# Seven products for the third column group of a gated ffn's first layer, interleaved with the other two groups

## The chip, the cores and the metric

One NeuronCore of one Trainium2 chip runs the whole program. The metric is device time in microseconds (us). Three executions of the kernel before took 1438.28, 1441.61 and 1444.34 us; the median is 1441.61 us.

## The reference

Threshold attention over 8 batches x 8 heads, 576 positions, head width 64, and then a feed-forward block with a product of two linear branches over the 4608 resulting rows. All data is float32.

```python
scores = scale * np.matmul(q, k.transpose(0, 1, 3, 2))
thresh = np.max(scores, axis=-1, keepdims=True) - tau
scores = np.where(scores >= thresh, scores, -1000000000.0)
scores = scores - np.max(scores, axis=-1, keepdims=True)
attn = np.exp(scores)
attn = attn / (np.sum(attn, axis=-1, keepdims=True) + 1e-09)
attn_out = np.matmul(attn, v)
...
x = attn_out.transpose(0, 2, 1, 3).reshape(B * S, H * D)   # 4608 x 512
a = x @ w_a                                                # 512 -> 1536
b = x @ w_b
return a * b @ w_out                                       # 1536 -> 512
```

## The kernel before

**Units and blocks.** The attention is cut into 160 units. A unit `(i, u)` is a pair of heads of one batch and up to two tiles of 64 query rows for each head. `scores` (line 386) makes the score products of a unit in two PSUM tiles, VectorE takes the row maximum (L393), ScalarE makes bias and exponential (L413, L414), VectorE thresholds, multiplies and sums (L417); only then are the two PSUM tiles free. ScalarE normalises (L436), VectorE transposes 32x32 pieces (L480), and two DMAs by way of a DRAM scratch finish the transposition (`swap`, `wT`). Three units later `weighted` multiplies with v (L520), and ScalarE and VectorE copy the result into a tile of x (L527, L528). When 256 rows of x are complete they are a block; there are 18.

**The matmuls.** All are 64x64 tiles of the array, four at a time in its four quadrants. A float32 matmul shows as two records in the trace.

**ffn of a block.** The 1536 columns of the hidden layer are three groups of 512. The second and third group are tile `h1` of the hidden values, the first is tile `h0`. For 16 of the blocks (all but the first two, which are plain throughout) the two groups of `h1` are computed by `sevens_of` (matmuls at L680): x is split by rows and depth, the weights by depth and branch, and seven products of such quarters (128 rows, half the depth) stand in place of eight, with sums of the weights that were made once on GpSimd (`first_sums`, L641) and sums of x that are made for each block (`x_sums`, L550, four per tile of x, written into a tile `xU`). Products 1, 6, 7 and 4 accumulate one on the other in one PSUM pair `a`; between them the running value is copied out (L698, L705, L710) or used (L714). Products 5 and 3 do the same in a pair `b` (L719, L723), product 2 has a `b` of its own (L702). The columns of `h0` are computed plainly (L753): four steps of 256 rows x 128 columns x two branches, and each evicts with ScalarE (L759) or VectorE (L761). Three of the plain steps stand between products of the seven, so that 6 and 7, 7 and 4, 5 and 3 are never neighbours. The second layer (L810) also uses seven products; its sums of hidden values run on GpSimd (L779).

**Order.** Every engine's order is fixed when the program is written (`keep_order`). A loop over slots `g` emits a unit's steps and, between them, calls `advance`, which takes steps from the generator `ffn` as long as a budget of matmul columns lasts. So the matmuls of a block stand spread over about nine units, and evictions of the ffn stand in the queues of ScalarE and VectorE between the steps of the attention. After the last unit the remaining blocks run alone.

**Memory.** PSUM is one pool of four pairs of banks (`banks`); scores of a unit take two, every product, `pv` and `po` takes one. Tiles of x, their half-swapped copies `xS` and the sums `xU` come from one pool of `XT_BUFS` = 7; temporaries `osb` (the `u3` of product 7 and the outputs of the second layer) from `OSB_BUFS` = 4; v of a head pair from four buffers, loaded once per pair.

**DMA.** Nearly all DMAs are issued by SyncE in one queue. In the loop they are put in a list `bulk` by `post`, and `passed`/`pump` take them from it in proportion to the matmul columns issued (`PUMP`), each tied to a matmul already issued; `flush` issues whatever a consumer needs at once. Entries `tw` and `wT` overtake others.

Of the kernel before, what the change touches and what calls it, by code (L numbers as in the profile page):

```python
# [24 lines left out]
XT_BUFS = 7  # L25
Q_BUFS = 2
OSB_BUFS = 4
# [7 lines left out]
RAWS = 4  # L35
# [19 lines left out]
def kernel(  # L55
# [83 lines left out]
    def post(key, *moves):  # L139

        if not state["paced"]:
            for move in moves:
                nc.sync.dma_start(*move)  # L143
        else:
            at = len(bulk)
            if key[0] in ("tw", "wT"):
                while at and bulk[at - 1][0][0] not in ("tw", "wT") and bulk[at - 1][1] >= state["slot"] - 1:
                    at -= 1
            bulk.insert(at, (key, state["slot"], moves))
# [50 lines left out]
    def load_v(i, again=False):  # L200
        b, hp = pairs[i]
        if not again:
            loaded[i]["v"] = loads.tile([P, NSLOT, D], FP32, tag="vm", bufs=HP, name="vm")
        for j in range(2):
            rows, half = v[b, 2 * hp + j], loaded[i]["v"][j * D:(j + 1) * D]
            if i >= HP or again:
                if i < HP:
                    rows = rows.rearrange("(c s p) d -> p c s d", c=2, p=Q)
                else:
                    rows = rows.rearrange("(p c s) d -> p c s d", c=2, p=Q)  # L210
                post(("v", i), *((half[c * Q:(c + 1) * Q], rows[:, c]) for c in range(2)))
            else:
                nc.sync.dma_start(half, rows.rearrange("(s p) d -> p s d", p=D))
# [37 lines left out]
    more_sb = more_u32.bitcast(FP32)  # L251

# [17 lines left out]
    def convert_first(n):  # L270

        if n not in raws:
            return
        raw, top = raws[n], pieces[n][0]
        if n % (OSB_BUFS + 1) == OSB_BUFS:
            low = more_sb[:, 2 * QUARTER + P:2 * QUARTER + P + CW]
        else:
            low = work.tile([P, CW], FP32, tag="osb", bufs=OSB_BUFS, name="low")
        nc.scalar.activation(top, raw[:, :, 1].bitcast(FP32), AF.Abs)
        nc.scalar.activation(low, raw[:, :, 0], AF.Copy, bias=2.0, scale=2.0 ** -51)
        stages[n] = low  # L290
# [35 lines left out]
    rooms = [t.rearrange("p (n w) -> p n w", n=NR) for t in rooms]  # L326
    load_rows(0, "q", rooms[0])
# [217 lines left out]
    def x_sums(x):  # L545

        t = x_tile("xU").rearrange("p m (k n) -> p m k n", k=2)
        b11, b12, b21, b22 = (x[:, k * 2:k * 2 + 2, n * P:(n + 1) * P] for k in range(2) for n in range(2))
        for m, a, b in ((0, b12, b11), (1, b22, t[:, 0]), (2, b22, b12), (3, b21, t[:, 1])):
            nc.gpsimd.tensor_tensor(t[:, m], a, b, op=ALU.subtract)  # L550
        return t

    def exchange_blocks():
        while complete and not state["layer"] and not blocks:
            x, what = complete.pop(0)
            xs, done = ahead.pop(what[1:], (None, 0)) if what[0] == "half" else (None, 0)
            xs = xs or x_tile("xS")
            for hp in range(done, HP):
                exchange(x, xs, hp, 0, HALF, nc.gpsimd)
            blocks.append(((x, xs) + ((x_sums(x), x_sums(xs)) if state["first"] >= 3 * SEVENS else ()), what))  # L560
# [70 lines left out]

    def first_sums(n, group):

        quarter = [w[:, NG - 1 - group].rearrange("p (z y e) w -> p z y (e w)", z=2, y=2)[:, :, y]
                   for w in (wa_sb, wb_sb) for y in range(2)]
        s1, s2, s4 = ((first_sb, more_sb)[group][:, m * QUARTER:(m + 1) * QUARTER].rearrange("p (z w) -> p z w", z=2)
                      for m in range(3))
        a11, a12, a21, a22 = quarter
        out, a, b, op = ((s1, a21, a22, ALU.add), (s2, s1, a11, ALU.subtract), (s4, a12, s2, ALU.subtract),
                         (a21, a11, a21, ALU.subtract))[n]  # L640
        nc.gpsimd.tensor_tensor(out, a, b, op=op)  # L641

    def sevens_of(x, hg, plain):
# [5 lines left out]

        def quarter(n, y):  # L650
            return [[(wa_sb, wb_sb)[n][:, NG - SEVENS + g, k] for k in (2 * y, 2 * y + 1, 2 * y + HP, 2 * y + HP + 1)]
                    for g in range(SEVENS)]

        def s(m):
            return [[(more_sb, first_sb)[g][:, m * QUARTER + k * CH:m * QUARTER + (k + 1) * CH] for k in range(HP)]
                    for g in range(SEVENS)]
# [4 lines left out]
        def of_t(m):  # L661
            return [z[:, m, e] for z in (t, ts) for e in range(2)]

        products = {1: (quarter(0, 0), of_x(0, 0)), 6: (s(1), of_t(1)), 7: (quarter(1, 0), of_t(2)),
                    5: (s(0), of_t(0)), 2: (quarter(0, 1), of_x(1, 0)), 4: (quarter(1, 1), of_t(3)),
                    3: (s(2), of_x(1, 1))}
        nf = 2 * SEVENS
        whole = nf * HP * P

        def product(m, out, fresh, last):  # L670
            w, moving = products[m]
            left = whole
            for f in range(nf):
                g, y = f // 2, f % 2
                for k in range(HP):
                    for r in range(2):
                        rows = slice(r * D, (r + 1) * D)
                        for c in range(2):
                            w0 = y * P + c * D
                            nc.tensor.matmul(out[c * D:(c + 1) * D, r, f * P:(f + 1) * P],  # L680
                                             w[g][k][rows, w0:w0 + D], moving[k][rows],
                                             start=(fresh and k == 0 and f == 0),
                                             stop=(k == HP - 1 and f == nf - 1),
                                             skip_group_check=True)
                    left -= P
                    if left:
                        yield P, left, whole
# [4 lines left out]
        h0, h1 = (hg[:, :, :, n * P:(n + 1) * P].rearrange("p f r n -> p r f n") for n in range(2))  # L692
        third = [work.tile([P, nf * P], FP32, tag="osb", bufs=OSB_BUFS, name="u3") for _ in range(2)]
        done = P, 0, 0

        a = banks(nf * P, "pab")
        yield from product(1, a, True, False)
        nc.scalar.copy(h0, split(a))  # L698
        yield done
        b = banks(nf * P, "pab")  # L700
        yield from product(2, b, True, True)
        nc.vector.tensor_tensor(h0, h0, split(b), op=ALU.add)  # L702
        yield done
        yield from product(6, a, False, False)
        nc.scalar.copy(h1, split(a))  # L705
        yield done
        yield from plain(0)
        yield from product(7, a, False, False)
        for r in range(2):
            nc.scalar.copy(third[r], a[:, r])  # L710
        yield done
        yield from plain(1)
        yield from product(4, a, False, True)
        nc.vector.tensor_tensor(h0, h0, split(a), op=ALU.mult)  # L714
        yield done
        b = banks(nf * P, "pab")
        yield from product(5, b, True, False)
        for r in range(2):
            nc.vector.tensor_tensor(third[r], third[r], b[:, r], op=ALU.add)  # L719
        yield done  # L720
        yield from plain(2)
        yield from product(3, b, False, True)
        nc.vector.tensor_tensor(h1, h1, split(b), op=ALU.add)  # L723
        for r in range(2):
            pool(h1[:, r], h1[:, r], third[r].rearrange("p (f n) -> p f n", n=P), op=ALU.mult)
        yield done

    def ffn(xT, what):
# [39 lines left out]
        if len(xT) == 4:  # L768
            rest = [(f, 0, HALF, (w,)) for f in range((NG - SEVENS) * n) for w in both]
            yield from sevens_of(xT, h_of[1], lambda k: plain(rest[k:k + 1]))  # L770
            yield from plain(rest[3:])
# [5 lines left out]
        if state["sums"]:  # L777
# [14 lines left out]

            def keep(name):
                return work.tile([P, 2, CH], FP32, tag="osb", bufs=OSB_BUFS, name=name)

# [3 lines left out]
            for both in ((1, 4), (2, 5), (7, 6), (3,)):  # L799
# [23 lines left out]
                if 3 not in both:  # L823
                    t = keep("kept")
# [14 lines left out]
                else:  # L839
                    t = keep("kept")[:, 0]  # L840
# [43 lines left out]
    def cost():  # L884

        return BLOCK_COLS - (NF // 2 * CH if state["sums"] else 0) - (SEVENS * 2 * HP * P if state["first"] >= 3 * SEVENS else 0)
# [3 lines left out]
    def advance(cols):  # L890
        running["owed"] += cols
        while running["owed"] > 0:
            if running["ffn"] is None:
# [4 lines left out]
                if len(blocks[0][0]) == 4 and state["first"] == 3 * SEVENS:  # L898
                    for group in range(SEVENS):
                        first_sums(3, group)  # L900
                    state["first"] += 1
                running["tiles"] = len(blocks[0][0])
# [25 lines left out]
    def make_x(count):  # L928

        while (len([k for k in x_of if k != (0, 0)]) + len(xtail_of) + len(ahead) + len(complete) + sum(len(x) for x, _ in blocks)  # L930
# [50 lines left out]
    for g in range(len(units) + PV_LAG):  # L981
# [92 lines left out]
        for p in range(1, NPR):  # L1074
            if g == first[p] - 1:
# [21 lines left out]
        if g > first[HP] + 1 and not converting and state["first"] < 3 * SEVENS:  # L1097
            first_sums(state["first"] % 3, state["first"] // 3)
            state["first"] += 1
# [39 lines left out]
```

## Time and profile before

| what | value |
|---|---|
| times of three executions | 1438.28, 1441.61, 1444.34 us |
| profiled execution, span from first to last instruction | 1439.3 us (no other time is given for it) |
| TensorE matmul busy | 1386.8 us, 96% |
| VectorE / ScalarE / GpSimd busy | 1015.6 / 683.9 / 480.4 us (71 / 48 / 33%) |
| DMA, SyncE's queue | 217.74 MB in 324160 packets, 58.5% of 16 engines |
| first-layer seven products, L680 | 27% of the chain that ended last |
| plain first-layer steps, L753 | 19% |
| second layer, L810 | 20% |

In rows of groups the first figure behind the bar is the time in which at least one of the group ran, the second the mean duration in ns of one, the third the idle time of the engine in front of them, with what ended it. In timelines the first two columns are start and duration in us. Up to about 130 us the weights are loaded and converted; from 240 us to 1280 us units and blocks are interleaved; after the last unit the rest of the ffn runs alone.

### The profile page before, as it was taken

To read this page: it belongs to the slowest core of one execution; us is meant where nothing else is said; L and a number is where in the kernel's file an instruction comes from. 1 tells how busy PE (TensorE), PEld (TensorE's weight loads), DVE (VectorE), ACT (ScalarE), POOL (GpSimd) and SP (SyncE) were. 2 spreads that over 40 slices of the span, in tenths; PEclk is the share of its full clock that TensorE was granted. 3 is DMA by queue.
4 is the path that set the end of the run, shared out by engine and by line. 5 is a ranking of instruction groups with operands and counts; after the bars stand their busy time and mean duration, and the time that the engine had idled before them with its cause. 6 is when DMAs were issued, how large, how long until landed. Compare 5 with 4: busy or idle time off the path is not lost.

```text
span 1439.3 us, 77100 instructions
## 1 busy us (share of the span) xinstructions
PE 1386.8 (96%) x34208; PEld 1282.4 (89%) x34208; DVE 1015.6 (71%) x2244; ACT 683.9 (48%) x1244; POOL 480.4 (33%) x668
## 2 busy tenths in 40 slices
PE   6888999999999999999999999999999999999998
PEld 5777798988879889989999999898898989999998
DVE  6997778788767877676757786778867776755223
ACT  5876455545545454544444545344535454430110
POOL 2763713415060605132333333240506060605000
PEclk9899999999999999999999999999999999999999
DMA  9975667667755776567545677466755686450000
GB/s 210 252 227 141 173 173 191 182 171 192 202 137 153 176 201 159 152 160 189 147 125 137 159 186 203 118 171 149 207 135 142 164 217 167 121 160 18 3 18 17
DMA packets 327004, 223.25 MB, mean 155 GB/s; under 512 B 171536, under 2 KB 310800, under 8 KB 326672
## 3 DMA queue, kind: packets, MB, share of 16 engines
q1 hardware_dynamic: 324160, 217.74, 58.5%
q8 instruction: 269, 4.41, 1.3%
q10 hardware_dynamic: 2512, 0.59, 0.2%
q14 instruction: 63, 0.52, 0.1%
HBM read 128.58 MB, written 89.65 MB: 152 GB/s over the span
## 4 chain that ended last, share of the span: by engine, by line
PE 88%; DVE 4%; DMA 4%; issue 2%; SPq 2%; ACT 1%; DVEq 0%; ACTq 0%
PE pab L680 27%; PE po L810 20%; PE pab L753 19%; PE sc L386 10%; PE pv L520 10%; PE po L856 1%; DMA wT<-swap 1%; PE tp L461 1%; DVE mx L393 1%; DVE tw L480 1%; SPq L197 1%; DMA raw<-in_moe_w_a_dram 1%; SPq L143 1%; DMA raw<-in_moe_w_b_dram 0%; DVE tw L417 0%
## 5 line engine op out<-in xcount | busy, mean ns | idle before, releaser
L436 ACT ACTIVATE tw<-tw,rcp 128x576 f32<-128x576 f32 x272 | 197.8, 769 | 228.7 <-DVE rcp L430 228.6
L393 DVE TENSOR_REDUCE mx<-sc 128x1 f32<-128x576 f32 x288 | 206.1, 752 | 140.7 <-PE sc L386 115.6
L414 ACT ACTIVATE tw<-sc,bias,scalars 128x576 f32<-128x576 f32 x288 | 239.4, 831 | 9.8 <-ACT bias L413 0.2
L646 POOL TENSOR_TENSOR h<-h,u 128x512 f32<-128x512 f32 x28 | 35.1, 1276 | 604.2 <-DVE h L723 465.4
L810 PE MATMUL po<-wo_sb,h 64*64 64x256 f32 x3264 | 230.8, 377 | 0.0
L417 DVE SCALAR_TENSOR_TENSOR tw<-sc,thr,tw 128x576 f32<-128x576 f32 x288 | 222.6, 797 | 9.7 <-ACT tw L414 9.1
L386 PE MATMUL sc<-kT,qT 64*64 64x288 f32 x2016 | 198.1, 405 | 7.2 <-issue 2.9
L480 DVE STREAM_TRANSPOSE tw<-tw 128x576 f32<-128x576 f32 x272 | 196.0, 754 | 0.8 <-ACT tw L436 0.8
L810 PEld LDWEIGHTS po<-wo_sb,h 64*64 64x64 f32 x3264 | 178.7, 133 | 15.8 <-DVE h L723 0.3
L520 PE MATMUL pv<-wT,vm 64*64 64x160 f32 (+3 forms) x5184 | 181.7, 273 | 7.1 <-issue 4.3
L520 PEld LDWEIGHTS pv<-wT,vm 64*64 64x64 f32 x5184 | 167.7, 134 | 13.9 <-issue 6.8
L810 PE MATMUL po<-sums_u,h 64*64 64x256 f32 x2448 | 169.6, 377 | 0.3 <-DVE h L761 0.3
L779 POOL TENSOR_TENSOR h<-h 128x256 f32<-128x256 f32 x168 | 117.4, 733 | 119.8 <-PE po L810 116.1
L386 PEld LDWEIGHTS sc<-kT,qT 64*64 64x64 f32 x2016 | 119.5, 133 | 31.9 <-issue 10.6
L810 PEld LDWEIGHTS po<-sums_u,h 64*64 64x64 f32 x2448 | 132.2, 133 | 12.5 <-DVE h L761 1.2
L680 PE MATMUL pab<-xU,wb_sb 64*64 64x128 f32 x4096 | 138.5, 270 | 0.1
L680 PEld LDWEIGHTS pab<-xU,wb_sb 64*64 64x64 f32 x4096 | 131.0, 133 | 2.2 <-issue 0.5
L413 ACT ACTIVATE bias<-mx,scalars 128x1 f32<-128x1 f32 x288 | 83.3, 289 | 92.5 <-DVE mx L393 92.3
L680 PE MATMUL pab<-xS,wa_sb 64*64 64x128 f32 x2048 | 113.1, 270 | 1.2 <-issue 1.2
L753 PE MATMUL pab<-xS,wb_sb 64*64 64x256 f32 (+1 forms) x1536 | 102.9, 359 | 4.1 <-issue 4.1
L527 ACT COPY xT<-pv 128x128 f32<-128x128 f32 (+1 forms) x68 | 17.6, 259 | 187.2 <-PE pv L520 152.6
L753 PE MATMUL pab<-xS,wa_sb 64*64 64x256 f32 (+1 forms) x1536 | 101.4, 361 | 0.0
(138 smaller groups left out, 2427.7 us busy)
## 6 DMA issues: line engine op xcount, KB each, us to landing
wT<-swap SPq DMA_DIRECT2D x244, 288.0 KB, 3.8
swap<-tw SPq DMA_DIRECT2D x480, 144.0 KB, 2.9
vm<-in_v_dram SPq DMA_DIRECT2D x128, 72.0 KB, 2.8
swap<-tw SPq DMA_DIRECT2D x128, 72.0 KB, 3.1
kT<-in_k_dram SPq DMA_DIRECT2D x112, 72.0 KB, 3.1
wT<-swap SPq DMA_DIRECT2D x56, 144.0 KB, 2.6
out_dram<-kept SPq DMA_DIRECT2D x30, 256.0 KB, 3.5
qT<-in_q_dram SPq DMA_DIRECT2D x112, 40.0 KB, 2.6
```

The lines of the kernel that those rows point to most:

```text
L386: nc.tensor.matmul(sc[j if u < NT else 0][to, c], qT[r, q0:q0 + D], kT[r, c * SH:(c + 1) * SH], start=True, stop=True)
L393: nc.vector.tensor_reduce(mx[:, c], sc[j], axis=AX.XY, op=ALU.max)
L413: nc.scalar.activation(bias[:, j:j + 1], mx[:, j:j + 1], AF.Copy, scale=e_nscale)
L414: nc.scalar.activation(wb[j], sb[j], AF.Exp, bias=bias[:, j:j + 1], scale=e_scale)
L417: nc.vector.scalar_tensor_tensor(out=wv, in0=sb[j], scalar=thr[:, j:j + 1], in1=wv, op0=ALU.is_ge, op1=ALU.mult, accum_out=sums[:, j:j + 1])
L436: nc.scalar.activation(w, w, AF.Copy, scale=rcp[:, j:j + 1])
L480: nc.vector.transpose(w, w)
L520: nc.tensor.matmul(pv[c * D:(c + 1) * D, y], vm[rows, s], wT[y](rows, s), start=(s == 0), stop=(s == NSLOT - 1))
L680: nc.tensor.matmul(out[c * D:(c + 1) * D, r, f * P:(f + 1) * P], w[g][k][rows, w0:w0 + D], moving[k][rows], start=(fresh and k == 0 and f ...
L753: nc.tensor.matmul(pab[c * D:(c + 1) * D, r], w[rows, f // n, k, fs + c * D:fs + (c + 1) * D], moving, start=(k == 0), stop=(k == H - 1))
L779: (nc.vector if state["over"] else nc.gpsimd).tensor_tensor(*a, **kw)
L810: nc.tensor.matmul(po[c * D:(c + 1) * D, r, y], ht[rows, t0:t0 + D], other[rows, f], start=(f == 0), stop=(f == NF // 2 - 1))
```

## The change

The first group (`h0`), until now plain, is computed by the same seven products for the same 16 blocks, as a second stream beside the one of the two other groups. `sevens_of` now has a stream `main` (two groups, products of 128 rows x 512 columns) and a stream `side` (one group, 128 rows x 256 columns), and their products alternate in a fixed order. Each stream keeps its own pair `a`, later its own pair `b`. The plain steps between products are gone from these blocks.

The weight sums of the new group are three further sums of 128x1024: one stays on chip (`kept_sb`), the two others are stored to DRAM once and loaded again into one tile (`side_sb`) in each block, in two halves each, as entries `s` of `bulk` that overtake others as `tw` and `wT` do. Room for this comes from: `xU` in a pool of its own with two tiles of three sums each, the fourth sum being written over the part of x that is no longer needed; `XT_BUFS` 7 to 5; `osb` 4 to 3 tiles; v in two buffers instead of four, loaded once for each half of a pair's units (and for two early pairs in an `xU` tile); staging of raw weights 4 to 3 tiles with `side_u32` as a further place. The weight sums are made two per slot instead of one.

```diff
-XT_BUFS = 7
+XT_BUFS = 5
...
-OSB_BUFS = 4
+OSB_BUFS = 3
...
-            if key[0] in ("tw", "wT"):
+            if key[0] in ("tw", "wT", "s"):
...
-        t = x_tile("xU").rearrange("p m (k n) -> p m k n", k=2)
+        t = work.tile([P, 3, 2, P], FP32, tag="xU", bufs=2, name="xU")
         b11, b12, b21, b22 = (x[:, k * 2:k * 2 + 2, n * P:(n + 1) * P] for k in range(2) for n in range(2))
-        for m, a, b in ((0, b12, b11), (1, b22, t[:, 0]), (2, b22, b12), (3, b21, t[:, 1])):
-            nc.gpsimd.tensor_tensor(t[:, m], a, b, op=ALU.subtract)
+        for out, a, b in ((t[:, 0], b12, b11), (t[:, 1], b22, t[:, 0]), (b12, b22, b12), (t[:, 2], b21, t[:, 1])):
+            nc.gpsimd.tensor_tensor(out, a, b, op=ALU.subtract)
...
+        if group == SEVENS and 1 <= n < 3:
+            post(("s", 2), (side_store[n - 1], side_sb))
+
+    def side_load(m):
+
+        for k in range(2):
+            part = slice(k * QUARTER // 2, (k + 1) * QUARTER // 2)
+            post(("s", m), (side_sb[:, part], side_store[m][:, part]))
...
+            if groups == (0,) and m in (6, 3):
+                flush(("s", 2), ("s", sums[m] - 1))
...
-        yield from product(6, a, False, False)
-        nc.scalar.copy(h1, split(a))
-        yield done
-        yield from plain(0)
-        yield from product(7, a, False, False)
...
+            def step(m):
+                if m == 1:
+                    a = held["a"] = banks(size, "pab")
+                    yield from product(1, groups, a, True, False)
+                    nc.scalar.copy(h0, split(a))
...
+                elif m == 5:
+                    b = held["b"] = banks(size, "pab")
+                    yield from product(5, groups, b, True, False)
+                    if len(groups) > 1:
+                        for r in range(2):
+                            nc.vector.tensor_tensor(third[r], third[r], b[:, r], op=ALU.add)
+                    else:
+                        u3 = both.rearrange("p (r n) -> p r n", r=2)
+                        nc.vector.tensor_tensor(u3, u3, b, op=ALU.add)
...
+        main, side = stream((1, 2), h_main), stream((0,), h_side)
+        for of, m in ((main, 1), (main, 2), (main, 6), (side, 1), (main, 7), (side, 6), (main, 4), (side, 7), (side, 2),
+                      (side, 4), (main, 5), (side, 5), (main, 3), (side, 3)):
+            yield from of(m)
...
-            rest = [(f, 0, HALF, (w,)) for f in range((NG - SEVENS) * n) for w in both]
-            yield from sevens_of(xT, h_of[1], lambda k: plain(rest[k:k + 1]))
-            yield from plain(rest[3:])
+            yield from sevens_of(xT, h_of[1], h_of[0])
...
-            if g == first[p] - 1:
+            if g == (first[p] - 1 if p < HP else first[p] + 1) or p >= HP and g == second[p] + 2:
                 load_v(p)
```

## The prediction

> **What bounds the kernel now.** First the page: busy time, then the chain that ended last.
>
> ```profile
> PE 1386.8 (96%) x34208; PEld 1282.4 (89%) x34208; DVE 1015.6 (71%) x2244; ACT 683.9 (48%) x1244; POOL 480.4 (33%) x668
> ...
> PE pab L680 27%; PE po L810 20%; PE pab L753 19%; PE sc L386 10%; PE pv L520 10%; PE po L856 1%; DMA wT<-swap 1%; PE tp L461 1%; DVE mx L393 1%; DVE tw L480 1%; SPq L197 1%; DMA raw<-in_moe_w_a_dram 1%; SPq L143 1%; DMA raw<-in_moe_w_b_dram 0%; DVE tw L417 0%
> ```
>
> TensorE is the bound; the 19% of L753 is what the change works on. Then the busy time by stretches (columns: stretch, length, PE, PEld, DVE, ACT, POOL, clock, DMA share, GB/s):
>
> ```profile
> 240.00:1280.00 1040.00, 1024.99 (x25760) 946.21 (x25754) 770.65 (x1714) 516.39 (x922) 343.50 (x510) 1.00 0.63 165
> 1280.00:1439.30 159.30, 153.50 (x3970) 153.00 (x3962) 56.95 (x106) 16.98 (x30) 21.67 (x34) 1.00 0.10 28
> ```
>
> In the long middle TensorE idles only 15 us, VectorE is 74% busy and the DMA engines 63%; at the end nothing but TensorE counts. The chain in order of time for one block of that end gives clean prices:
>
> ```profile
> 1320.66 10.26 PE pab L680 x374
> ...
> 1331.19 3.20 PE pab L753 x57
> ...
> 1334.60 3.27 PE pab L680 x118
> ...
> 1338.14 3.20 PE pab L753 x57
> ...
> 1341.55 6.77 PE pab L680 x246
> ...
> 1348.58 3.20 PE pab L753 x57
> ...
> 1358.98 17.87 PE po L810 x331
> ```
>
> From 1320.66 to 1358.98, 38.32 us: seven products and four plain steps. A plain step takes 3.41 (1331.19 to 1334.60), so a product takes (38.32 - 4 x 3.41)/7 = 3.53. Last, VectorE around product 5 of a block in the middle, the matmul that follows, and the same place in the end:
>
> ```profile
> 614.17 1.42 DVE L393 TENSOR_REDUCE mx<-sc 128x1 f32<-128x576 f32 x2 [1.38 <-PE pab L680]
> 615.63 0.23 DVE L394 TENSOR_SCALAR thr<-mx,scalars 128x2 f32<-128x2 f32 x1
> 615.76 1.43 DVE L480 STREAM_TRANSPOSE tw<-tw 128x576 f32<-128x576 f32 x2
> 617.12 1.25 DVE L719 TENSOR_TENSOR u<-u,pab 128x512 f32<-128x512 f32 x2
> ```
> ```profile
> 618.42 0.67 PE L680 MATMUL pab<-xT,more_u 64*64 64x128 f32 x16 [0.20 <-DVE u L719]
> ```
> ```profile
> 1348.65 1.28 DVE L719 TENSOR_TENSOR u<-u,pab 128x512 f32<-128x512 f32 x2 [2.22 <-PE pab L680]
> ```
>
> Product 5 ended at 614.77; its two adds stood behind a unit's maxima and transposes and ended 3.60 us later, and product 3 waited 0.20 us for them, although a whole plain step lay between. Undisturbed the adds end 1.36 us after the product. This is where the change cuts the cover.
>
> **The change part by part.** All against the profiled execution, span 1439.3 us, 2.3 us under the median of the three runs.
>
> *Matmuls, -24.* Per block four plain steps go (13.64 us) and seven side products of 64 records come. By columns (8 become 7) that is 11.94, a gain of 1.71 per block and 27.3 for 16. By the row above a product of 128 records takes 3.53, half of it 1.77, seven 12.36: a gain of 1.28, or 20.5. The truth lies between, as part of the 3.53 is the change from one form to the other; I take 24. In the changed order 9.8 of the 27.3 by columns falls behind the last unit, where nothing else runs.
>
> The Trainium skill, "TensorE: Matmul & The Clock Gate", section "Back-to-back issue gap", speaks against the change: sustained pairs of weight load and matmul at 81 ns for 128 columns and 131 ns for 512, so that narrow matmuls are dear. An estimate from that page alone (98 ns at 256 by a straight line) makes seven narrow steps cost 7 x 81 against 4 x 98, 45% more than the plain ones, or +98 us over 16 blocks. The trace does not agree: in this row 128 records of width 128 take 3.53 us and 64 of width 256 take 3.41.
>
> *Product 5 to 3, +13.* VectorE must finish both adds before main 3 continues on the same pair. Before, a plain step (3.41) or more lay between; now it is side 5, 1.71 us of columns, in 10 of the 14 blocks that run beside units, and 2.67 to 4.11 in four. In the timeline of before the adds of these 14 ended 2.37, 3.14, 3.52, 3.37, 3.60, 1.41, 1.39, 3.35, 3.36, 5.18, 3.57, 3.02, 2.05 and 1.43 us after the product. What exceeds 1.71 is 17.7 together, 1.27 a block: 10 x 1.27 + 1 for the four others = 13.7. Bounds: 0 (1.36 is under 1.71, if VectorE were free) and 18.
>
> *Products 6 to 7, 7 to 4, side 7 to 4, +5.* ScalarE's copies likewise. L705 ended 1.05 to 1.08 us after product 6 in ten of the 14 blocks, 1.75 to 4.32 in four; the excess over 1.71 is 0.37 a block, and six blocks have only side 1 between, four 2.2 to 2.7: 3. L710 ended 1.2 after product 7, in two blocks 3.1: 1.5 with the same counting, and 1 for side 7. Bounds 0 and 10.
>
> *PSUM, +9.* Two of the four pairs are now held from side 1 through main 4 without a break, so the other two serve scores and pv. In the middle the second threshold (L417) of a unit ended on average 4.1 us after its last score matmul for the first tile and 4.9 for the second. In the orders of the two programs, from the first such block to the last unit, I counted the matmul time (columns at 0.417 ns, from 3.41 us for a plain step) between the last score into a pair and the next first write to it: under 5.0 us before 14 times, together 10.6 short; after 37 times, 22.2 short; against 4.6 us, 5.5 and 10.5. So 5 to 12, I take 6. Scores right behind pv in the same pair (under 1 us between, where copies L527 and L528 took 1.0): 11 before, 17 after, 2; `po` behind main 3 with only side 3 between, 1. Bounds 0 and 17.
>
> *Second layer, +2.* Its second product needs main's hidden values: add 1.2 (VectorE), two multiplications of 1.28 (GpSimd). Side 3, one product and two steps lie in front, 5.1 us instead of 6.8. Bounds 0 and 5.
>
> *DMAs, +1.* 64 side loads of 256 KB, 112 loads of v of 72 KB, two stores: 26 MB on 217.7, so the share of 0.63 in the middle becomes 0.7. The side loads overtake q, k and v and stand in SyncE's queue ahead of later `swap` and `wT`. They are due 15 and 17 us of matmuls after they are posted, against 3.8 us from issue to landing of a 288 KB `wT` group, and TensorE waited only 0.4 us for `wT` in all. If that margin went, each of 64 pv would pay up to the 1 to 2 us such a load takes; bounds 0 and 6. v's second load comes three slots of 8 us ahead of its use.
>
> *At nothing.* VectorE gains three operations of 0.67 a block, 32 us, and ScalarE one of 0.58; VectorE comes to 78% in the middle; that shows only in the waits above. GpSimd's weight sums (one more 2.37 in place at the first such block) hide behind products 1, 2, 6 of main; 3 us if not. Conversion: one raw buffer fewer but `side_u32` more, six places for `low` instead of five; -2 to +2.
>
> *Overlap, -10.* The waits add to 30. They share units: a TensorE that stood 2 us for VectorE finds the scores' pair free afterwards, and the bursts of waiting already in the middle (15 us idle) are partly the same. I take off a third; bounds 0 and -15.
>
> Sum: -24 + 13 + 5 + 9 + 2 + 1 - 10 = -4: 1435 for the span, 1437 against the median.
>
> **The rivals.** *The covers hold.* If VectorE's queue falls otherwise around side 5 and the pairs suffice, the waits cost some 8 instead of 20 us: -27 + 1.5 + 8 = -17, 1424. For it: in five of 14 blocks L719 ended within 2.4 us; against it: the 0.20 us wait at 618.42 with twice the cover.
>
> *Slower: PSUM.* If a unit's chain from score to threshold lengthens by 0.6 us, because three more evictions a block stand in VectorE's queue, the shortfall at 5.5 us counts: 46 after against 23 before, +23 in place of +6, with the waits for product 3 at 15 and little overlap: -24 + 15 + 5 + 26 + 2 + 1 - 12 = +13, 1455. It decides as soon as the waits exceed 24 us in all. For it: VectorE at 78%; against it: TensorE's idle time of 15 us, so the present margins do hold.
>
> *The gain is not there* because the middle is VectorE's: the evictions of 13 blocks, 26 us, would then lengthen it, less the 9.8 after the last unit: +16, 1458. Against it: VectorE idles 26% there.
>
> **How the numbers follow.** About 0.5%, 7.2 us, is what a measurement of this kernel tells from no change. The forecast (1428 to 1447) has 0.46, the covers 0.27, slower 0.27 with both its mechanisms. About 0.12 of the forecast lies under 1434.4, and 0.01 over 1448.8: faster 0.39, same 0.33, slower 0.28. The range 1420 to 1456 reaches to the middle of both rivals; the likeliest case alone has 1428 to 1447.
>
> **What would show it.** L753 in the 16 blocks gone, TensorE busy down by 20 to 27; idle time of TensorE in the middle up from 15 to 30 or more, put down to VectorE's add after main 5 and to L417 ahead of scores; the stretch after the last unit 8 to 10 us shorter; `wT` and side loads absent from TensorE's waits. Wrong would be: side loads late (TensorE waiting for DMA), or an idle time no larger than now, which makes it the first rival.

## The result, and the profile after

The changed kernel takes 1509.2 us (median of 4 runs, 1505.1 to 1512.0), the kernel before on the same chip 1443.0 us: a ratio of 1.0464 with a 95% interval of 1.0434 to 1.0493. It is slower by some 67 us, where 1437 us, a little faster, was forecast. The medians of the kernel before move between 1443 and 1448 us from one group of runs to the next, so below every size is taken from ratios, at 1446 us for 1.

The page of the changed kernel (busy time, the instruction queue, the chain that ended last):

```profile
PE 1392.6 (93%) x37280; PEld 1253.0 (83%) x37280; DVE 1044.2 (69%) x2280; ACT 692.2 (46%) x1260; POOL 500.2 (33%) x684
...
q8 instruction: 294, 4.82, 1.4%
...
PE 74%; DVE 10%; DMA 6%; issue 5%; ACT 2%; SPq 2%; POOL 1%; DVEq 0%; ACTq 0%; POOLq 0%
PE pab L706 33%; PE po L864 17%; PE sc L397 9%; PE pv L531 8%; PE pab L812 5%; DVE mx L404 2%; DVE tw L491 2%; PE po L910 1%; DVE tw L428 1%; SPq L143 1%; DMA kT<-in_k_dram 1%; DMA raw<-in_moe_w_a_dram 1%; DMA wT<-swap 1%; DVE u L763 1%; DMA swap<-tw 1%
```

Of the kernel before, its instruction queue and the chain by engine:

```profile
q8 instruction: 269, 4.41, 1.3%
...
PE 88%; DVE 4%; DMA 4%; issue 2%; SPq 2%; ACT 1%; DVEq 0%; ACTq 0%
```

L706 is the new line of the seven products, L812 the plain steps that are left (first two blocks). TensorE carries 3072 more matmuls and as many more weight loads, although it has fewer columns to move, and its share of the chain falls from 88% to 74%; VectorE's rises from 4% to 10% and "issue", time in which TensorE waited for nothing that the profile shows, from 2% to 5%. No single wait took the 67 us.

Busy time by stretches of the changed kernel, the same long middle and what comes after it (stretch, length, PE, PEld, DVE, ACT, POOL, clock, DMA share, GB/s):

```profile
240.00:1280.00 1040.00, 973.46 (x26827) 879.49 (x26822) 753.14 (x1652) 491.78 (x881) 322.51 (x475) 1.00 0.66 177
1280.00:1504.70 224.70, 212.61 (x6014) 199.57 (x6007) 102.53 (x206) 50.35 (x89) 54.44 (x83) 1.00 0.28 80
```

In the middle TensorE idles 66.5 us instead of 15, at a clock of 1.00 as before. VectorE is busy 72% of it, no more than before, so its amount of work is not the bound. What TensorE and VectorE waited for, of the changed kernel (engine, tile, line, then what it waited for: us in total, times, longest):

```profile
PEld pab L706 <- issue: 31.7, 48, 2.0
...
PEld sc L397 <- issue: 20.1, 34, 2.5
...
PE pab L706 <- issue: 17.5, 24, 1.5
...
DVE qT L365 <- DMA qT<-in_q_dram: 16.3, 10, 6.1
DVE kT L365 <- DMA kT<-in_k_dram: 15.9, 8, 3.3
...
PEld pab L706 <- DVE u L763: 13.7, 8, 2.9
...
PE pab L706 <- DVE u L763: 11.4, 8, 2.6
...
PE po L864 <- DVE h L775: 3.8, 5, 1.3
PE po L864 <- DVE h L770: 3.6, 3, 2.1
```

And of the kernel before, in the same view:

```profile
DVE kT L354 <- DMA kT<-in_k_dram: 9.6, 9, 2.7
...
DVE qT L354 <- DMA qT<-in_q_dram: 4.9, 5, 1.8
...
PEld pab L680 <- issue: 4.7, 11, 1.2
...
PE pab L680 <- issue: 2.2, 4, 1.0
```

Three things above all are new or larger: "issue" waits inside the products, the wait of main product 3 for VectorE's add (L763), which was forecast, and VectorE's waits for late q and k loads, twice as long. A fourth is missing: the gain itself. The last two blocks, where nothing but TensorE works, in the chain of the changed kernel in order of time (start us, us, what):

```profile
1384.92 7.88 PE pab L706 x283
1392.80 0.85 issue
1393.65 10.94 PE pab L706 x384
1404.59 0.10 issue
1404.69 3.72 PE pab L706 x128
1408.41 0.29 issue
1408.71 15.38 PE pab L706 x546
...
1424.20 18.09 PE po L864 x333
1442.29 7.31 PE pab L706 x265
...
1480.57 15.57 PE po L864 x287
```

From 1384.92 to 1424.09 the first layer takes 39.2 us, in the last block, to 1480.46, 38.2. Before it was 38.32, so seven eighths of the columns take as long as all of them or longer, with no other engine in the way.

Where the loss arises, from the start of each unit's first score in the two traces: the changed kernel is level with the kernel before at unit 32 of 160, 13 us behind at 64, 30 at 96, 56 at 128, 68 at 159, and 65 at the end. Nothing is lost in the conversion of the weights; from the first block with seven products on, the loss grows steadily.

### The profile page after: what moved, and what is told of

Same layout as the page of the kernel before. It is cut to its first block, busy times and chain, and to the rows that moved or that the text cites. A ratio compares the mean times of both kernels' runs of the same rounds, so it can differ in the third digit from the quotient of the medians.

```text
span 1504.7 us, 83661 instructions
## 1 busy us (share of the span) xinstructions
PE 1392.6 (93%) x37280; PEld 1253.0 (83%) x37280; DVE 1044.2 (69%) x2280; ACT 692.2 (46%) x1260; POOL 500.2 (33%) x684
## 3 DMA queue, kind: packets, MB, share of 16 engines
q8 instruction: 294, 4.82, 1.4%
## 4 chain that ended last, share of the span: by engine, by line
PE 74%; DVE 10%; DMA 6%; issue 5%; ACT 2%; SPq 2%; POOL 1%; DVEq 0%; ACTq 0%; POOLq 0%
PE pab L706 33%; PE po L864 17%; PE sc L397 9%; PE pv L531 8%; PE pab L812 5%; DVE mx L404 2%; DVE tw L491 2%; PE po L910 1%; DVE tw L428 1%; SPq L143 1%; DMA kT<-in_k_dram 1%; DMA raw<-in_moe_w_a_dram 1%; DMA wT<-swap 1%; DVE u L763 1%; DMA swap<-tw 1%
## 5 line engine op out<-in xcount | busy, mean ns | idle before, releaser
L864 PEld LDWEIGHTS po<-wo_sb,h 64*64 64x64 f32 x3264 | 165.8, 134 | 27.1 <-DVE h L770 4.4
L864 PE MATMUL po<-sums_u,h 64*64 64x256 f32 x2448 | 159.1, 377 | 3.8 <-DVE h L775 3.8
L706 PE MATMUL pab<-xS,wa_sb 64*64 64x128 f32 x3072 | 151.8, 270 | 1.1 <-issue 1.1
L397 PEld LDWEIGHTS sc<-kT,qT 64*64 64x64 f32 x2016 | 110.3, 133 | 51.1 <-issue 16.4
L836 POOL TENSOR_TENSOR h<-h 128x256 f32<-128x256 f32 x180 | 125.8, 732 | 45.3 <-PE po L864 43.9
L864 PEld LDWEIGHTS po<-sums_u,h 64*64 64x64 f32 x2448 | 120.3, 133 | 24.1 <-DVE h L775 6.8
L706 PE MATMUL pab<-xT,wa_sb 64*64 64x128 f32 x2688 | 134.8, 270 | 5.1 <-DVE h L757 3.1
L706 PEld LDWEIGHTS pab<-xS,wa_sb 64*64 64x64 f32 x3072 | 125.5, 133 | 2.2 <-issue 1.6
L706 PEld LDWEIGHTS pab<-xT,wa_sb 64*64 64x64 f32 x2688 | 110.8, 133 | 8.7 <-DVE h L757 3.6
L706 PE MATMUL pab<-xU,wb_sb 64*64 64x128 f32 x3072 | 100.8, 270 | 6.7 <-issue 2.7
```

Source lines behind the costliest of these rows:

```text
L397: nc.tensor.matmul(sc[j if u < NT else 0][to, c], qT[r, q0:q0 + D], kT[r, c * SH:(c + 1) * SH], start=True, stop=True)
L836: (nc.vector if state["over"] else nc.gpsimd).tensor_tensor(*a, **kw)
L864: nc.tensor.matmul(po[c * D:(c + 1) * D, r, y], ht[rows, t0:t0 + D], other[rows, f], start=(f == 0), stop=(f == NF // 2 - 1))
```

## The experiments

Four theories. *Theory 1, instruction supply:* TensorE's instructions arrive in fetches (294 of 4.82 MB in all, so 16 KB each; 37280 matmul records and as many weight loads, so some 254 in a fetch). A matmul of 128 columns uses up its records twice as fast per column as one of 256. *Theory 2:* waits for evictions and PSUM pairs, the forecast's own. *Theory 3:* the buffers and loads, that is v read twice, streamed sums and fewer temporaries. *Columns:* the saving itself, 27 us by columns.

**Narrow plain steps in the kernel before.** The 256-column matmuls of the plain group of the 16 blocks are cut into two of 128; columns, order, buffers and loads stay.

```diff
-for c in range(2):
-    nc.tensor.matmul(pab[c * D:(c + 1) * D, r],
-                     w[rows, f // n, k, fs + c * D:fs + (c + 1) * D], moving,
-                     start=(k == 0), stop=(k == H - 1))
+parts = 2 if len(both) == 1 else 1
+for half in range(parts):
+    wide = slice(half * P, (half + 1) * P) if parts == 2 else slice(0, c1 - c0)
+    for c in range(2):
+        nc.tensor.matmul(pab[c * D:(c + 1) * D, r, wide],
+                         w[rows, f // n, k, fs + c * D:fs + (c + 1) * D], moving[:, wide],
+                         start=(k == 0 and half == 0), stop=(k == H - 1 and half == parts - 1),
+                         skip_group_check=(parts == 2))
```

> The kernel before, with each 256-column matmul of the plain first-layer steps of the 16 blocks cut into two of 128 columns: the same columns, results, evictions, PSUM pairs, buffers and DMAs, but 4096 more matmul records and as many weight loads. Theory 1 (TensorE's instructions do not arrive fast enough when matmuls are 128 columns wide: in the changed kernel 63 of the waits with no releaser, 37 us, end 1.2 to 1.6 us after a 16 KB instruction fetch): slower by 25 to 70 us, near 1485, with idle time put down to issue. Theory 2 (lost cover: evictions and PSUM pairs): no change, 1442 within 5. Theory 3 (fewer buffers, v twice, side loads): no change.

Measured: 1486.1 us, ratio 1.0286 (1.0257 to 1.0315), 41 us more. The waits of this kernel (L756 holds the plain matmuls cut in two, L680 the seven products, which are as they were):

```profile
PEld pab L756 <- issue: 17.4, 28, 1.8
...
PEld pab L680 <- issue: 15.4, 25, 1.9
...
PE pab L756 <- issue: 12.3, 15, 1.6
...
PE pab L680 <- issue: 9.3, 17, 1.7
```

Cutting the plain matmuls also made the untouched products at L680 wait (before: 4.7 and 2.2; the waits of the plain steps themselves, 8.9 and 7.8, lay ahead of 240 us there). In the kernel before, one to three narrow products had a wide plain step behind them, and that was cover for the instruction stream, not only for VectorE. Theory 1 is confirmed in size. Matmuls and weight loads are doubled together, so the time alone doesn't tell the fetches from the weight loads; the traces do. From 240 us on, all 27 of this kernel's "issue" waits before a first-layer matmul, and 46 of 47 before a weight load, end 1.15 to 1.65 us after an instruction fetch has landed. In the changed kernel it is 24 of 24 and 44 of 48.

**The first group plain, all else as changed.** Buffers, v read twice, streamed sums and their loads stay; the first column group is computed by plain steps between the products as before. (Its plain steps read the quarter of x that GpSimd has overwritten, so the outcome is not the reference's.)

```diff
-for of, m in ((main, 1), (main, 2), (main, 6), (side, 1), (main, 7), (side, 6), ...):
-    yield from of(m)
+for m, step in ((1, None), (2, None), (6, 0), (7, 1), (4, None), (5, 2), (3, 3)):
+    yield from main(m)
+    ...
+    if step is not None:
+        yield from plain(step)
```

> The changed kernel with its buffers, v loaded twice and the side loads, but the first group computed by plain steps of 256 columns between the products, as before (one more plain step behind product 4 is not there, the order is that of before). The plain steps read a part of x and of the weights that has been replaced by a difference, so the values of that group differ; the work is the same. Theory 1 and theory 2: near the kernel before, 1442 within 8. Theory 3: most of the loss remains, 1480 or more.

Measured: 1476.9 us, ratio 1.0212 (1.018 to 1.0245), 31 us above the kernel before. Theories 1 and 2 alone had 1442 within 8 here, so neither is the whole cause, and theory 3 had 1480 or more: the loads and buffers that were priced at 1 us cost 31, before a single side product runs.

**All matmuls of the products joined to 256 columns.**

> The changed kernel with the matmuls of all its first-layer products joined in pairs: one matmul of 256 columns in place of two of 128, so the same columns into the same PSUM places with half the instructions; the second half of the columns is multiplied with the wrong weights and the wrong half of x, everything else (order, evictions, waits, buffers, DMAs) stays. Theory 1: 50 to 70 us faster than the changed kernel, 1440 to 1460, the rest being the waits for evictions that were forecast. Theory 2: within 10 us of the changed kernel, 1500 to 1510. Theory 3: the same as theory 2.

Measured: 1501.0 us, ratio 1.0385, 11 us under the changed kernel by ratios. "Issue" waits at the products fell (31.7 to 13.1 before weight loads, 17.5 to none before matmuls), but this kernel read the quarter of x that GpSimd overwrites in place, in products that the changed kernel computes without it, and waited for it. Its waits:

```profile
PE pab L729 <- POOL xT L567: 17.6, 4, 5.5
```

That wait is the experiment's own, so the run settles nothing. It was repeated with tiles and quarters that each product has at hand:

```diff
+def x_wide(k, n):
+    return [z[:, k * 2:k * 2 + 2, n * P:(n + 1) * P] for z in (x, xs) for e in range(2)]
...
+if WIDE(groups) and y:
+    left -= P
+    if left:
+        yield P, left, whole
+    continue
...
-nc.tensor.matmul(out[c * D:(c + 1) * D, r, f * P:(f + 1) * P],
-                 w[g][k][rows, w0:w0 + D], moving[m][k][rows],
+to = out[c * D:(c + 1) * D, r, f * P:(f + n) * P]
...
+nc.tensor.matmul(to,
+                 w[g][k][rows, w0:w0 + D], m2[rows],
...
```

> The changed kernel with every pair of 128-column matmuls of the seven products joined to one of 256 columns (half as many matmul and weight-load records for the same columns); both halves of the columns now go by the first half's weights and over two neighbouring blocks of x or of a temporary, so the computation of the first layer is not the reference's. Unlike the earlier joined kernel it reads the very tiles and quarters that each product of the changed kernel reads or a neighbour that is ready by then. Theory 1 (the instructions of 128-column matmuls come no faster than TensorE uses them, so every hiccup stays): 35 to 41 us below the changed kernel's 1509, that is 1468 to 1475, with TensorE's 'issue' waits near 6 us in all. Rival (the loss is waits for PSUM, VectorE and late loads, and only moves): above 1495.

Measured: 1478.9 us, ratio 1.021 (1.0174 to 1.0246): 37 us less than the changed kernel by ratios, 30 by medians. (`WIDE` is true throughout, `n` is 2 and `m2` is `wide[m][k]`.) The forecast of this run, 1468 to 1475, was 4 us too low. The waits of this kernel:

```profile
PEld pab L732 <- DVE u L789: 20.5, 10, 3.5
...
PE pab L732 <- DVE u L789: 16.2, 9, 3.0
...
PEld pab L732 <- issue: 12.7, 21, 3.0
```

"Issue" falls from 31.7 to 12.7, and none of these 21 waits follows a fetch by 1.15 to 1.65 us any more, while the wait for VectorE's add rises from 13.7 to 20.5: part of the time given back went to the next wait. On the other hand joining also takes away the little supply loss that the kernel before had in its own products, and the columns themselves get slightly cheaper (27.4 ns for 128 in the rows before, half of 54 ns here, some 9 us of the 37). Two runs from opposite sides, +41 and -37, agree in size.

**The changed kernel without the loads of the streamed sums.**

```diff
-for k in range(2):
-    part = slice(k * QUARTER // 2, (k + 1) * QUARTER // 2)
-    post(("s", m), (side_sb[:, part], side_store[m][:, part]))
+pass
```

> The changed kernel without the 64 side loads of 256 KB (the products that use the two streamed sums read whatever is left in the tile). Theory 1: up to 10 us faster, because an instruction fetch meets fewer data transfers. Theory 2: no change, within 3 us. Theory 3: 20 us faster or more.

Measured: 1496.4 us, ratio 1.035 (1.0327 to 1.0374), 16 us less than the changed kernel, between what theories 1 and 3 gave. In the changed kernel's trace TensorE never waited for a streamed sum; the same removal was therefore made in the two other settings.

**The same in the kernel with the plain first group.**

> The earlier kernel with the changed buffers and loads but a plain first group, now without the 64 loads of streamed sums, which nothing reads there. Theory 3a (the loads cost because they stand ahead of q and k in the paced list): 10 to 15 us below the 1477 of that kernel, 1462 to 1467, still 15 to 20 above the kernel before, which is then v read twice and the fewer buffers. Theory 3b (the side loads cost only where a side product waits for them): 1474 to 1480.

Measured: 1464.8 us, ratio 1.0123 (1.0093 to 1.0154), 13 us less than with the loads, and no product there could wait for them. Theory 3a has the time right: the loads cost by being in the way. VectorE's waits for q and k are 38.1 us with them and 27.0 without.

**The same with the joined matmuls.**

> The changed kernel with the joined matmuls of the mended run and without the 64 loads of the streamed sums (both together; the first layer is not the reference's). If instruction supply (30 us by the mended run) and side loads (13 us by the run without them) add: 1463 to 1470. If one covers the other: 1475 to 1482, no better than the mended run alone. What stays above the kernel before at 1448 is then v read twice, temporaries and waits for the evictions of the products, less 27 us of saved columns.

Measured: 1460.9 us, ratio 1.0104 (1.0072 to 1.0136), 15 us under the joined kernel: the two parts add. This kernel's end also shows what the columns are worth when nothing holds them up. Its chain in order of time:

```profile
1384.00 18.04 PE po L888 x335
1402.04 36.26 PE pab L730 x672
```

The whole first layer of a block in 36.26 us, against 39.2 and 38.2 with 1344 narrow matmuls and 38.32 before.

**v read twice in the kernel before.** One line:

```diff
-            if g == first[p] - 1:
+            if g == first[p] - 1 or p >= HP and g == second[p] + 2:
                 load_v(p)
```

> The kernel before with one line changed: the v of the 28 later pairs is loaded a second time, as in the changed kernel, and nothing else. Theory 3c (what remains of the buffer part without the streamed sums, 17 us over the kernel before in the earlier run, is v read twice: 56 more posts in the paced list ahead of q and k): 1457 to 1466. Rival 3d (the second v loads are covered; the 17 us come from the fewer temporaries, two buffers in place of three and four): 1444 to 1451.

Measured: 1468.5 us, ratio 1.015 (1.0096 to 1.0205), 22 us more (14 to 30 by the interval) for 112 loads of 72 KB, somewhat above what theory 3c gave. Its waits:

```profile
DVE kT L354 <- DMA kT<-in_k_dram: 24.9, 10, 5.8
...
DVE qT L354 <- DMA qT<-in_q_dram: 14.6, 10, 3.7
...
PE sc L386 <- DVE xt L528: 8.5, 2, 4.3
...
PE pv L520 <- DMA wT<-swap: 4.4, 1, 4.4
```

VectorE's waits for q and k rise from 14.5 to 39.5 us. VectorE's order is fixed by the program, so a conversion of q that waits for its load holds the thresholds and evictions behind it; scores waited 8.5 us for an eviction at L528, 1.2 before. The kernel with all the changed buffers and v read twice, but without streamed sums, stood 18 us above the kernel before, no more than this one: the fewer temporaries show no cost of their own. The transposed weights `wT`, for which TensorE waited next to nothing before, come late too.

**Can the price be taken away by giving q and k out earlier?** Twice in the kernel before with v read twice: all loads given out faster, and q and k put ahead of v and the stores.

```diff
-PUMP = 320
+PUMP = 220
```
```diff
+            elif key[0] in ("q0", "k", "q1"):
+                while at and bulk[at - 1][0][0] in ("v", "o"):
+                    at -= 1
             bulk.insert(at, (key, state["slot"], moves))
```

> The kernel before with v read twice (1468.5 us in the earlier run) and PUMP 220, so that the paced list gives out its loads faster. Theory 3e (the second v loads cost because q, k and the transposed weights behind them in the list come late): VectorE's waits for q and k fall from 39 us to under 15 and the time to 1448 to 1456. Theory 3f (the added transfers themselves cost, by what they share with the other transfers and the instruction fetches): the waits fall and the time stays at 1462 to 1470.

> The kernel before with v read twice and the q and k loads put ahead of v loads and of stores in the paced list; PUMP stays 320, so as many bytes are given out per column of TensorE's work. Theory 3e: 1450 to 1460. Theory 3f: 1463 to 1470.

Measured: 1461.2 us, ratio 1.0104 (1.0071 to 1.0137), and 1459.6 us, ratio 1.007 (1.0043 to 1.0098): 7 and 12 us less than with v twice alone, though the intervals of the first overlap and those of the second barely touch. VectorE's waits for q and k fell to 14.9 and 14.4 us, the level of the kernel before, yet 10 to 15 us stay. The waits of the second:

```profile
PE pv L523 <- DMA wT<-swap: 8.8, 4, 4.0
DVE kT L357 <- DMA kT<-in_k_dram: 8.3, 4, 2.9
```

With q and k first, `wT` is what comes late (8.4 us with PUMP 220). The truth lies between the two theories: by the middle values a third to a half of the price went when q and k came in time, the rest stays. Whether that rest is all `wT` was not isolated.

**The same edits in the changed kernel (there q and k also go ahead of the streamed sums), and in the kernel before as controls.** Each alone in the changed kernel; in the kernel before PUMP 220 alone, then both.

> The changed kernel with PUMP 220 in place of 320: the paced list gives out its loads faster, so the q and k loads are issued earlier and none is forced out as too old. Theory 3 (late q and k loads hold VectorE's in-order queue, and the thresholds behind it): VectorE's waits for q and k fall from 32 us to under 15, and the time falls by 8 to 20 us, to 1489 to 1501. Rival (those waits are covered by the first layer's matmuls): the waits fall and the time stays within 4 us of 1509.

> The changed kernel with the q and k loads put ahead of v loads, stores and streamed sums in the paced list. Theory 3e: VectorE's waits for q and k fall from 32 us to under 18 and the time by 8 to 20 us, to 1489 to 1501. Theory 3f, or a cover by the narrow matmuls: 1504 to 1512.

> The kernel before with PUMP 220 in place of 320, the control. Theory 3: its waits for q and k are 14.5 us, and at the same exchange as in the changed kernel (half or so of the waits on the path) it gains 3 to 8 us: 1436 to 1444. Rival (waits covered): 1445 to 1449.

> The kernel before with the q and k loads ahead of v loads and stores in the paced list, and PUMP 220: the control, and the one version that could beat the kernel before. With 14.5 us of waits for q and k there and PUMP alone at 1446 against 1448: 1440 to 1447 by theory 3e; 1445 to 1449 by theory 3f.

Measured: in the changed kernel 1519.2 us (ratio 1.048, 1.0426 to 1.0533) and 1521.0 us (1.0496, 1.0452 to 1.0539), no better than 1.0464 and by medians 10 and 12 us worse; in the kernel before 1446.2 us (0.9976, 0.9955 to 0.9998) and 1445.8 us (0.999, 0.9959 to 1.0022). The expected gain of 8 to 20 us did not come. The waits of the changed kernel with PUMP 220:

```profile
PEld pab L706 <- issue: 46.8, 71, 2.2
...
PE pab L706 <- issue: 27.2, 41, 1.9
...
DVE kT L365 <- DMA kT<-in_k_dram: 13.5, 5, 4.4
...
DVE qT L365 <- DMA qT<-in_q_dram: 8.0, 7, 2.0
```

The waits for q and k fell from 32.2 to 21.5 us (18.0 with q and k first), and "issue" at the products rose from 31.7 to 46.8 and from 17.5 to 27.2: where one wait went, the narrow stream's own limit took its place. Whether the faster loads also delay the fetches was not isolated. The best version found is the kernel before with PUMP 220, ahead by 0.2%, at the edge of what such runs can tell.

**The changed kernel without the adds of main product 5.**

```diff
-for r in range(2):
-    nc.vector.tensor_tensor(third[r], third[r], b[:, r], op=ALU.add)
+pass
```

> The changed kernel without the two VectorE additions that follow the main product 5 and that product 3 waits for (the sum with product 5 is left out, so the outcome is not the reference's). The forecast priced this wait at 13 us and the trace shows 13.3 us before the product 3. If that wait is on the path: 1494 to 1500, 9 to 15 below the changed kernel. Rival (another wait takes its place, the eviction of product 3 or the next block's): 1503 to 1509.

Measured: 1504.0 us, ratio 1.0396 (1.0336 to 1.0455): 5 us by medians, 10 by ratios, with overlapping intervals, so the expected 9 to 15 came at most in part. The 13.3 us that TensorE stood at the entry of main product 3 are gone from the trace (0.3 us are left). The waits of this kernel:

```profile
PEld pab L706 <- issue: 42.6, 62, 1.6
...
PE pab L706 <- issue: 25.3, 41, 1.4
```

Again "issue" took over part of it, 31.7 to 42.6. By theory 1, instructions catch up while TensorE stands for another reason, and run out sooner without that pause. So the wait for product 5 was real, and by itself worth less than its length. (The edit also takes 28 adds off VectorE, so even the 5 to 10 us are not all this wait.)

## Why the prediction was wrong

The account by ratios: columns -27 (worked out, as in the forecast), instruction supply +37 to +41, streamed sums +13 to +16, v read twice +22. With 39 and 15 that makes +49. The two load parts need not add: together, in the kernel with the plain first group, they cost 31, which makes +43. What is left to the measured +67, some 18 to 24 us, is a difference and was not measured by itself. The traces say what it can be: from 240 us on, counted from start to start of neighbouring matmuls, TensorE stood some 100 us in the changed kernel and 24 before, 33 of them (6 before) with "issue" right after a fetch, 42 (9 before) behind VectorE and 12 (4 before) behind ScalarE.

- *What bounds the kernel* was right: TensorE, and a change in its stream decides. But "busy" hid that TensorE's stream has a limit of its own. TensorE's busy time was to fall by 20 to 27 us; it rose by 6.
- *Matmuls, -24*: the step that failed most. As a price of columns it was near: by the row of before a narrow matmul takes 27.4 ns (10.26 us for 374), so 1344 of them 36.9 us, 1.4 less than the 38.32 of before, or 23 for 16 blocks. What the term put at nothing is that the stream of narrow matmuls stops. Its rows came from bursts of at most 374, each with a wide step behind it, and were taken for 1344 in a row. The blocks of the end took 39.2 and 38.2 us, and in the first the chain breaks at "issue" behind 384 and behind 128 matmuls, about what three fetches and one fetch bring; there 128 take 3.72 us. In the middle the loss comes as standstills of up to 2 us. The term was not -24 but about +12 (columns -27, supply +39). The 3.53 us for a product against 3.41 for a plain step was no sign of this: the joined kernel's 36.26 us for 672 matmuls make 3.45 for a plain step of 64, and then the row of before leaves 3.50 for a product, so most of the difference was a plain step taken too short.
- *The rule set aside.* The Trainium skill, "TensorE: Matmul & The Clock Gate", "Back-to-back issue gap", holds narrow matmuls to be dear, and the forecast answered that the trace did not agree. The estimate from its 81 ns, +98 us, is indeed far above the +41 of the narrow plain steps. Its direction came out right, but not as a higher price for every narrow matmul: in the bursts 128 columns cost 27.4 ns, half of a joined matmul 27.0, and the loss came as pauses.
- *DMAs, +1, bounds 0 to 6*: failed, measured +13 to +16 for the streamed sums and +22 for v. The working asked whether TensorE would wait for `wT` or a side load, as it had waited 0.4 us before. The profile of before held the other question: VectorE already waited 14.5 us for q and k, which stand in the same paced list, so anything put ahead of them had no margin there. With v twice `wT` itself lost its margin in the kernel before.
- *Product 5 to 3, +13*: the wait came as forecast, at L763, and TensorE stood 13.3 us at the entry of main product 3 over 14 blocks. As a part of the time it was worth less: without the adds the kernel gained 5 to 10.
- *Products 6 to 7, 7 to 4, side 7 to 4, +5*: somewhat low; the entries cost some 8 us together, within the bounds of 0 to 10.
- *PSUM, +9; second layer, +2; overlap, -10*: no run took them away. The second layer was above its bounds of 0 to 5 in the trace, some 7 us (the two rows of `po` above) where the kernel before had 0.3. The chain from the last score to the second threshold lengthened by 0.3 us (last tile of a unit: 4.74 to 5.06), half of what the PSUM rival needed. All wait terms but the DMAs summed to +19 with the overlap; the difference above is 18 to 24. That agreement is not a proof, as the parts of the account each carry some 4 us.
- *Overlap*: the idea that one wait covers another was right, and fits the run without the adds; but the cover taken away there was the supply's, which the sum did not contain.
- *The rivals*: none had the cause. "Slower: PSUM" had the sign, at 1455. "The middle is VectorE's" falls: VectorE is busy 72% of the middle, 74% before.
- *What would show it*: the two marks named as contrary were a TensorE waiting for DMA, or no more idle time. Neither came; the wait for DMA was VectorE's. TensorE's idle time in the middle rose as forecast, and further (66.5 us), but scores waited no longer for L417 (4.4 us, 6.0 before). The end got no 8 to 10 us shorter but only some 3 (68 behind at the last unit, 65 at the end).
- *The range*, 1420 to 1456, was built from the bounds of the priced terms. Two terms lay far outside theirs, both on the slow side: the matmuls', because its bounds came from bursts, and the loads', because it was bounded by a single consumer that showed no wait before.

## What to carry to other kernels

Count instructions as well as columns: halving the width of matmuls doubles the rate at which TensorE uses instructions, and in this kernel a stream of 128-column matmuls stayed near its price only where wide ones followed. A price read from short bursts holds for the long stretch that a change makes only if nothing runs dry in between: here 374 narrow matmuls ran without a pause, and 1344 did not. Before adding a load, look at every engine's waits for loads in the same queue, and price it by the one with the smallest margin.

## What the runs showed of the hardware

TensorE's instructions come in blocks of 16 KB, some 254 records each, by a queue whose fetches go with its records: 269 in the kernel before, 294 in the changed one, 210 in the joined one with its 26528 matmuls. In the narrow stretch of the changed kernel's end from 1391 to 1424 us they started 3.62 us apart on average (3.37 to 4.08), where 127 matmuls at 27.4 ns would take 3.48. In the first-layer products, from 240 us on, all 24 "issue" waits before a matmul and 44 of 48 before a weight load ended 1.15 to 1.65 us after a fetch had landed; in the joined kernel there were none before a matmul, and 21 of another timing before weight loads. Those before scores mostly did not follow a fetch (5 of 22 before weight loads). A single fetch took no longer than before (1.12 us on average in both), so why the next block comes too late is not shown. That the fetches are the mechanism is read from this timing; what the runs show directly is that the same columns in half the instructions cost 37 us less, and in twice the instructions 41 us more. Also unexpected: 8 MB of added reads, spread over a millisecond at a DMA share that went from 0.63 to 0.65, cost 22 us in a kernel whose TensorE had waited for almost no load.
